# Packed attention and two wide layers on one core: a reciprocal from another pair of ScalarE functions, one wait less, and a new list order

## The chip, the cores and the metric

One core of one Trainium2 chip runs the whole program. The metric is the device time of one execution in microseconds; three executions of the kernel before were timed, and one more was profiled.

## What is computed

Shapes: `q`, `k`, `v` are (8, 8, 576, 64), `p` is (8, 8, 32, 64); both layers have 4608 tokens, width 512 and hidden width 2048, all float32.

```python
p_packed = softmax(p k^T / 8) v              # 32 packed rows per head
x = softmax(q p_packed^T / 8) p_packed       # (4608, 512) after the heads are joined
h = x @ w_in1                                # layer 1
P = a0 + a1*h + a2*h^2 + a3*h^3
Q = 1 + |b0|*|h| + |b1|*h^2
x = (P / (Q + 1e-6)) @ w_out1
h = x @ w_in2                                # layer 2
out = (h * cos(h)) @ w_out2
```

## The kernel before

The program is a list of steps, each with an engine, an assumed duration, a key and the objects it reads and writes. `Plan.order` walks through the list as a model of five engines would: it starts, on each engine, the step with the lowest key among those that could start within 60 ns of the first, and the resulting order is the order in which instructions are recorded. A key is a place in a schedule written by hand (`at`, `FROM + u * UNIT`, ...) plus an entry of the table `WANTED` for its kind of step. So a new table means a new order on every engine; the engines then run their own queues strictly in that order and wait on each other by semaphores.

**Attention** runs in 16 units (`attention`, half the heads of one batch each): loads of `p`, `k`, `q`, `v`; PE transposes (L470); scores (L499); softmax of the packed queries (`exp1`, L517); the product with `v` (L550); the second scores; the second softmax (`exp2`, L590) with VectorE transposes around it; a store of the result.

**Weights** arrive as 64-bit words and are turned into a high and a low float32 part: `w_load` (512 KB), `w_exp` and `w_low` on ScalarE (L359, L362), `w_abs` and `w_join` on VectorE (L368, L378), then for most a rounding on ScalarE (L385) and a subtraction on GpSimd (L390). `raw` has two buffers, so a load waits for the `w_join` two conversions earlier. Layer 1 has 32 such conversions.

**Layer 1** has 128 items (`item1`; 16 token columns by 8 pairs of hidden blocks). The attention matrix is multiplied into the weights first (`m_prod`, L694; `m_hi`, L703; `m_lo`, L707). One item then is: `front` on PE (L739, 12 matmuls of 288 columns); on ScalarE `absolute` (L850), `lin` (L836), `slope` (L853); on GpSimd `denom` (L859); on VectorE `cubic` twice (L845, L847); on ScalarE `rsqrt` (L862) and `square` (L866), which make 1/Q; on VectorE `over` twice (L870) and `ratio` (L874); then `upper` on ScalarE (L902), `lower` on VectorE (L905) and `back` on PE (L776, 24 matmuls). `lower` is the seventh VectorE step of an item and the last thing that its `back` needs. The hidden values sit in one of two PSUM buffers (`b2`), which come free when the second `cubic` has read them; `V` and `U` have three buffers each, `T` four.

`rsqrt` of the first eight items waits for the end of every softmax: in `item1` it has `after=exps if j < 8 else ()`, where `exps` lists all `exp1` and `exp2` steps. `rsqrt` and the exponential are in different table sets of ScalarE.

**Layer 2** has 144 items (`item2`): `front` (L755), `lin` (L838), `rounded`, two `reduced`, `clipped`, `cosine` (L893), `times` (L896), `upper`, `lower`, `back`. Here the PSUM buffer is held until `times` has read it.

Of the kernel before, what the change touches and what calls it, by code (L numbers as in the profile page):

```python
# [14 lines left out]
AF = mybir.ActivationFunctionType  # L15
# [12 lines left out]
class Plan:  # L28
# [13 lines left out]
    WANTED = {  # L42
        "a2_hi": 440, "a2_lo": 373, "a2_load": -22, "absolute": -628, "back 0": 104, "back 1": 169,
        "clipped": 70, "copied k": 251, "copied q": 43, "cosine": 245, "cubic 0": 228,
        "cubic 1": -452, "denom": -187, "done1": -328, "done2": -87, "doubled": 357, "exp1": 189,
        "exp2": 14, "exp_copied 0": -32, "exp_copied 1": 522, "front 0": -261, "front 1": -372,
        "keep_attn": 271, "keep_out": 425, "keep_pack": 48, "less_max2": -596, "lin 0": -168,
        "lin 1": -278, "load k": 275, "load p": -435, "load q": -220, "load v": 93, "lower 0": -109,
        "lower 1": 78, "m_hi": -93, "m_lo": 32, "m_load": -254, "m_prod": -307, "max1": -559,
        "max2": -95, "open_left": -187, "open_right": 541, "over 0": 72, "over 1": 202, "pack": 436,  # L50
        "packed": -313, "ratio": -102, "recip1": 165, "recip2": 77, "reduced 0": 285,
        "reduced 1": -222, "rounded": 209, "rsqrt": 308, "scaled2": 49, "scores 0": -225,
        "scores 1": 191, "slope": -116, "square": -380, "store": 355, "sum2": 21, "taken p": -208,
        "taken pp": 108, "times": -128, "trans k": 275, "trans q": 147, "turn2": 46,
        "turn_back": -404, "turn_exp": 79, "turned p": 64, "turned pp": 562, "upper 0": -141,
# [6 lines left out]
        "x_load": -33, "x_out": -508,  # L62
    }
# [138 lines left out]
def pack_attention_moe_moe_kernel(  # L202
# [14 lines left out]
    nc = tc.nc  # L217
# [23 lines left out]
    ONE_EPS = 1.0 + 1e-6  # L241
    MAGIC = 12582912.0
    C1 = 6.28125
    C2 = 2 * PI - C1
    EARLY = 8
    N1 = NH * NPR
# [62 lines left out]
    add = plan.add  # L309
# [15 lines left out]
    cst = POOL["cp"].tile([P, 4], F32, name="cst")  # L325
# [285 lines left out]
    exps, ld_users, tp_users, ps_users = [], [], [], []  # L611
# [102 lines left out]
    def layer(j):  # L714
        return items[j][0]
# [110 lines left out]
    def shaped(j, nm):  # L826
        t = TILE[nm, j]
        return t.rearrange("p (a b) -> p a b", a=2) if layer(j) == 0 else t[:, 0:CH]
# [31 lines left out]

    def rsqrt(j):
        nc.scalar.activation(shaped(j, "V"), shaped(j, "U"), AF.Abs_reciprocal_sqrt, bias=ONE_EPS)  # L862

    def square(j):
        V = shaped(j, "V")
        nc.scalar.activation(V, V, AF.Square)  # L866

# [8 lines left out]
    def rounded(j):  # L876
        T = shaped(j, "T")
        return nc.vector.tensor_scalar(T, T, MAGIC, MAGIC, op0=ALU.add, op1=ALU.subtract)  # L878

    def reduced(j, e):  # L880
        T, Y = shaped(j, "T"), shaped(j, "U")
        if e == 0:
            return nc.vector.scalar_tensor_tensor(Y, T, -C1, hidden(j), op0=ALU.mult, op1=ALU.add)
        else:
# [27 lines left out]
    def at(j):  # L912
        return BEGIN + (ITEM1 * j if j <= N1 else ITEM1 * N1 + ITEM2 * (j - N1))
# [28 lines left out]
    W2P = ([P, 2 * HS], F32)  # L942
    fronts, rsqrts = {}, []
    HOMES2 = {f: f"s{f}" for f in range(NF // 2)}
# [28 lines left out]
    def item1(j):  # L973
        l, c, i = items[j]
        key = at(j)
# [8 lines left out]
        add("DVE", 730, key, cubic, j, 1, tail=85, r=[("h", j)], w=[("T", j)])  # L984
        rsqrts.append(add("ACT", 590, key, rsqrt, j, tail=105, r=[("U", j)], w=[("V", j)], after=exps if j < 8 else ()))
        add("ACT", 585, key, square, j, tail=100, w=[("V", j)])
        add("DVE", 669, key, over, j, 1, tail=85, r=[("V", j)], w=[("U", j)])
# [27 lines left out]
    def item2(j):  # L1015
        l, c, f = items[j]
        key = at(j)
# [5 lines left out]
        add("DVE", 336, key, clipped, j, tail=85, w=[("U", j)])  # L1023
        add("ACT", 535, key, cosine, j, tail=100, w=[("U", j)], after=rsqrts[-8:] if j < N1 + 8 else ())
        add("DVE", 600, key, times, j, tail=85, r=[("U", j), ("h", j)], new=[("V", ("V", j), *W2P)])
# [14 lines left out]
    for c in range(NH):  # L1040
        operands1(c)
        for i in range(NPR):
            j = c * NPR + i
# [20 lines left out]
    nc.sync.dma_start(par[:, 4:6], rat_b.unsqueeze(0).to_broadcast([P, 2]))  # L1064
    nc.vector.memset(cst[:, 0:1], ONE_EPS)
    nc.vector.memset(cst[:, 1:2], 0.25)
    nc.vector.memset(cst[:, 2:3], PI / 2)
    nc.scalar.activation(par[:, 4:6], par[:, 4:6], AF.Abs)
    for s in plan.order():
# [40 lines left out]
```

## Time and profile before

| | |
|---|---|
| three timed executions | 1664.0, 1664.95, 1667.54 us; median 1664.95 us |
| the profiled execution | 1665.34 us; span from first to last instruction 1663.4 us |
| busy, share of the span | PE 1570.7 us (94%), VectorE 1289.6 us (78%), ScalarE 1021.1 us (61%), GpSimd 308.3 us (19%) |
| mean granted TensorE clock | 0.97 of full speed |

The span is the sum of what an engine does and of what it waits. A stage in which PE is busy all the time is bound by PE; in one where PE waits, the question is which engine's work, or which chain across engines, it waits for. Numbers of rows and columns in names (`128x576`) are partitions by elements. L followed by a number is a line of the kernel before; in the changed kernel the lines after the table of constants are one higher.

### The profile page before, as it was taken

How to read it: one execution, taken by the hardware profiler on the slowest of the kernel's cores; microseconds unless marked ns; L12 is line 12 of the kernel's file. 1: busy time of each engine (PE TensorE's matmuls, PEld its weight loads, DVE VectorE, ACT ScalarE, POOL GpSimd, SP SyncE). 2: the span in 40 equal slices, each digit the busy share in tenths (PEclk: the TensorE clock that was granted, in tenths of full speed). 3: DMA queues.
4: the chain of work that ended last, by engine and by line, in shares of the span. 5: the costliest groups of instructions: out<-in, count | busy, mean ns of one | idle time of the engine just before them, and what ended most of it. 6: DMA issues, size and time to landing. Idle time of an engine off the chain costs nothing.

```text
span 1663.4 us, 26699 instructions
## 1 busy us (share of the span) xinstructions
PE 1570.7 (94%) x10176; PEld 1347.7 (81%) x10176; DVE 1289.6 (78%) x2025; ACT 1021.1 (61%) x1706; POOL 308.3 (19%) x246
## 2 busy tenths in 40 slices
PE   5876579999999999999999999999999999999998
PEld 3444278999999999999998888888888888888887
DVE  2655888999999999999998876667676667576664
ACT  3655788989999889898986543333333334333332
POOL 0233423333333333333322100000000000000000
PEclk7888689999999999999999999999999999999999
DMA  8998441212121121213153210101010100101010
GB/s 254 244 279 241 130 124 36 69 36 75 46 71 64 41 70 54 70 48 132 34 183 104 87 47 13 38 14 38 1 46 12 27 18 20 32 14 38 1 26 26
DMA packets 84383, 120.75 MB, mean 73 GB/s; under 512 B 19232, under 2 KB 61216, under 8 KB 84256
## 3 DMA queue, kind: packets, MB, share of 16 engines
q1 hardware_dynamic: 83872, 118.53, 24.4%
q8 instruction: 80, 1.31, 0.3%
q10 hardware_dynamic: 384, 0.52, 0.1%
q14 instruction: 47, 0.39, 0.1%
HBM read 85.99 MB, written 33.03 MB: 72 GB/s over the span
## 4 chain that ended last, share of the span: by engine, by line
PE 86%; DVE 4%; DMA 4%; ACT 3%; issue 1%; POOL 1%; SPq 1%; POOLq 0%; ACTq 0%
PE acc L776 46%; PE b L755 24%; PE b L739 11%; DMA raw<-in_moe_w_in_dram 2%; PE b L694 2%; PE b L470 1%; DMA v_in<-in_v_dram 1%; DMA raw<-in_moe_w_out_dram 1%; PE b L499 1%; DVE sc L368 1%; DVE T L870 0%; ACT sc L362 0%; DVE U L870 0%; POOL r L602 0%; ACT sc L359 0%
## 5 line engine op out<-in xcount | busy, mean ns | idle before, releaser
L776 PE MATMUL acc<-gh,wo 128*128 128x288 f32 x2048 | 418.0, 298 | 9.0 <-ACT gh L902 9.0
L776 PE MATMUL acc<-wo,gh 128*128 128x512 f32 x1152 | 354.7, 389 | 0.0
L776 PEld LDWEIGHTS acc<-gh,wo 128*128 128x128 f32 x2048 | 331.3, 189 | 26.9 <-issue 15.9
L776 PE MATMUL acc<-gl,wo 128*128 128x288 f32 x1024 | 303.2, 296 | 0.9 <-DVE gl L905 0.7
L776 PEld LDWEIGHTS acc<-wo,gh 128*128 128x128 f32 x1152 | 216.2, 188 | 44.9
L859 POOL TENSOR_TENSOR U<-U,V 128x576 f32<-128x576 f32 x128 | 182.7, 1437 | 361.4 <-DVE T L874 105.5
L776 PE MATMUL acc<-wo,gl 128*128 128x512 f32 x576 | 224.2, 389 | 0.0
L893 ACT ACTIVATE U<-U 128x512 f32<-128x512 f32 x144 | 90.6, 630 | 204.6 <-DVE U L889 204.5
L905 DVE TENSOR_TENSOR gl<-V,gh 128x512 fp32r<-128x512 f32 x144 | 99.2, 689 | 127.6 <-PE acc L776 126.2
L776 PEld LDWEIGHTS acc<-gl,wo 128*128 128x128 f32 x1024 | 194.4, 190 | 2.0 <-DVE gl L905 1.9
L838 ACT ACTIVATE T<-b 128x512 f32<-128x512 f32 x144 | 85.9, 596 | 176.7 <-PE b L755 176.4
L902 ACT CAST gh<-V 128x512 fp32r<-128x512 f32 x144 | 89.4, 621 | 73.4 <-PE acc L776 68.0
L776 PEld LDWEIGHTS acc<-wo,gl 128*128 128x128 f32 x576 | 108.1, 188 | 22.5
L905 DVE TENSOR_TENSOR gl<-T,gh 128x576 fp32r<-128x576 f32 x128 | 111.8, 876 | 7.6 <-PE acc L776 4.7
L878 DVE TENSOR_SCALAR T<-T 128x512 f32<-128x512 f32 x144 | 60.8, 423 | 70.2 <-ACT T L838 69.8
L896 DVE TENSOR_TENSOR V<-U,b 128x512 f32<-128x512 f32 x144 | 98.2, 682 | 18.0 <-ACT U L893 14.4
L853 ACT ACTIVATE U<-V,par 128x576 f32<-128x576 f32 x128 | 111.0, 873 | 0.8 <-DVE T L874 0.7
L870 DVE SCALAR_TENSOR_TENSOR T<-T,par,V 128x576 f32<-128x576 f32 x128 | 105.2, 841 | 5.0 <-ACT V L866 4.9
L836 ACT ACTIVATE T<-b,par 128x576 f32<-128x576 f32 x128 | 106.1, 830 | 3.5 <-PE b L739 3.0
L885 DVE SCALAR_TENSOR_TENSOR U<-T,U 128x512 f32<-128x512 f32 x144 | 103.6, 720 | 4.0
L850 ACT ACTIVATE V<-b 128x576 f32<-128x576 f32 x128 | 82.9, 648 | 35.4 <-PE b L739 26.3
L847 DVE SCALAR_TENSOR_TENSOR T<-T,par,b 128x576 f32<-128x576 f32 x128 | 101.3, 809 | 3.5 <-ACT V L850 1.4
(182 smaller groups left out, 3053.5 us busy)
## 6 DMA issues: line engine op xcount, KB each, us to landing
raw<-in_moe_w_out_dram SPq DMA_DIRECT2D x32, 512.0 KB, 3.7
q_in<-in_q_dram SPq DMA_DIRECT2D x16, 576.0 KB, 5.6
k_in<-in_k_dram SPq DMA_DIRECT2D x16, 576.0 KB, 6.8
x<-ob SPq DMA_DIRECT2D x16, 576.0 KB, 3.5
raw<-in_moe_w_in_dram SPq DMA_DIRECT2D x32, 256.0 KB, 4.3
v_in<-in_v_dram SPq DMA_DIRECT2D x64, 128.0 KB, 6.1
raw<-in_moe_w_in_dram SPq DMA_DIRECT2D x16, 512.0 KB, 4.8
w<-sc SPq DMA_DIRECT2D x32, 256.0 KB, 2.3
```

The lines of the kernel that those rows point to most:

```text
L739: nc.tensor.matmul(TILE["h", j][:, e, 0:HS], lhsT=w[:, o : o + P], rhs=x[:, g, :], start=n == 0, stop=n == 3 * NG - 1,)
L755: nc.tensor.matmul(h, lhsT=w[:, ks], rhs=x, start=n == 0, stop=n == 3 * KC - 1)
L776: nc.tensor.matmul(o, lhsT=w, rhs=x, start=i == 0 and n == 0, stop=i == last and n == len(todo) - 1,)
L836: nc.scalar.activation(T, hidden(j), AF.Identity, scale=par[:, 3:4], bias=par[:, 2:3])
L847: nc.vector.scalar_tensor_tensor(T, T, par[:, 1:2], h, op0=ALU.add, op1=ALU.mult)
L853: nc.scalar.activation(shaped(j, "U"), shaped(j, "V"), AF.Identity, scale=par[:, 5:6], bias=par[:, 4:5])
L859: return nc.gpsimd.tensor_tensor(Q, Q, V, op=ALU.mult)
L870: return nc.vector.scalar_tensor_tensor(t, t, add_, shaped(j, "V"), op0=ALU.add, op1=ALU.mult)
L885: return nc.vector.scalar_tensor_tensor(Y, T, -C2, Y, op0=ALU.mult, op1=ALU.add)
L893: nc.scalar.activation(Y, Y, AF.Sin, bias=PI/2)
L896: nc.vector.tensor_tensor(shaped(j, "V"), shaped(j, "U"), hidden(j), op=ALU.mult)
L905: return nc.vector.tensor_tensor(shaped(j, "gl"), result(j), shaped(j, "gh").bitcast(F32), op=ALU.subtract)
```

## The change

Three things change. The reciprocal: `rsqrt` then `square` become `log` then `inverse`, 1/Q as exp(-ln Q), with Q scaled by 2^-22 ahead of the logarithm and scaled back in the exponential's bias. The wait: `log` no longer has the `after=exps`. The table: every entry of `WANTED` is new, and `exp_copied` has one entry in place of two. A table set that holds logarithm and exponential is named ahead of the program.

```diff
     WANTED = {
-        "a2_hi": 440, "a2_lo": 373, "a2_load": -22, "absolute": -628, "back 0": 104, "back 1": 169,
+        "a2_hi": -487, "a2_lo": 16, "a2_load": -116, "absolute": -171, "back 0": 868,
...
-    def rsqrt(j):
-        nc.scalar.activation(shaped(j, "V"), shaped(j, "U"), AF.Abs_reciprocal_sqrt, bias=ONE_EPS)
-
-    def square(j):
+    def log(j):
+        nc.scalar.activation(shaped(j, "V"), shaped(j, "U"), AF.Ln, scale=2.0**-LOW, bias=cst[:, 0:1])
+
+    def inverse(j):
         V = shaped(j, "V")
-        nc.scalar.activation(V, V, AF.Square)
+        nc.scalar.activation(V, V, AF.Exp, scale=-1.0, bias=cst[:, 3:4])
...
-        rsqrts.append(add("ACT", 590, key, rsqrt, j, tail=105, r=[("U", j)], w=[("V", j)], after=exps if j < 8 else ()))
-        add("ACT", 585, key, square, j, tail=100, w=[("V", j)])
+        logs.append(add("ACT", 590, key, log, j, tail=105, r=[("U", j)], w=[("V", j)], ))
+        add("ACT", 585, key, inverse, j, tail=100, w=[("V", j)])
...
-        add("ACT", 535, key, cosine, j, tail=100, w=[("U", j)], after=rsqrts[-8:] if j < N1 + 8 else ())
+        add("ACT", 535, key, cosine, j, tail=100, w=[("U", j)], after=logs[-8:] if j < N1 + 8 else ())
...
-    nc.vector.memset(cst[:, 0:1], ONE_EPS)
+    nc.scalar.preload_act_table_set("natural_log_exp_and_others")
+    nc.vector.memset(cst[:, 0:1], ONE_EPS * 2.0**-LOW)
...
+    nc.vector.memset(cst[:, 3:4], -LOW * math.log(2.0))
```

What the new table does is seen in the order of the engines. Three places follow; the number behind a name tells one tile from the next of its kind.

**ScalarE, the reciprocal of layer 1's first item.** Before (`V_2347` is the first item's, `V_2359` the second's; `r_2364` is the last unit of attention):

```order
L590 ACTIVATE r_2364<-r_2364 128x576
L862 ACT_TABLE_LOAD
L862 ACTIVATE V_2347<-U_2354 128x576
L359 ACTIVATE sc_2450<-raw_2417 128x512
L362 ACTIVATE sc_2453<-raw_2417 128x512
L866 ACTIVATE V_2347<-V_2347 128x576
L862 ACTIVATE V_2359<-U_2379 128x576
```

In the change (`V_2348` first item, `V_2361` second, `V_2419` third, `r_2372` the last unit):

```order
L863 ACTIVATE V_2348<-U_2356,cst 128x576
L867 ACTIVATE V_2348<-V_2348,cst 128x576
L360 ACTIVATE sc_2412<-raw_2364 128x512
L363 ACTIVATE sc_2415<-raw_2364 128x512
L851 ACTIVATE V_2419<-b_1_2397 128x576
L837 ACTIVATE T_2425<-b_1_2397,par 128x576
L854 ACTIVATE U_2428<-V_2419,par 128x576
L863 ACTIVATE V_2361<-U_2383,cst 128x576
L867 ACTIVATE V_2361<-V_2361,cst 128x576
L591 ACTIVATE r_2372<-r_2372 128x576
```

The reciprocals of the first two items now stand ahead of the last exponential of attention, and no table load stands between them. Over the whole program ScalarE has three table loads before (at the start, here, and at the first cosine) and two now (at the start and at the first cosine).

**VectorE, the first item's `ratio` and `lower`.** Before (`T_2351` is the first item's, `sc` and `s` are weight conversions):

```order
L874 SCALAR_TENSOR_TENSOR T_2351<-U_2354,T_2351 128x576
L368 SCALAR_TENSOR_TENSOR sc_2519<-sc_2516,sc_2519 128x512
L870 SCALAR_TENSOR_TENSOR U_2379<-U_2379,V_2359 128x576
L378 SCALAR_TENSOR_TENSOR s_2533<-raw_2483,sc_2519 128x512
L905 TENSOR_TENSOR gl_2535<-T_2351,gh_2528 128x576
```

In the change (`T_2352` is the first item's, `T_2367` the second's, `T_2425` the third's):

```order
L871 SCALAR_TENSOR_TENSOR U_2356<-U_2356,V_2348 128x576
L379 SCALAR_TENSOR_TENSOR s_2417<-raw_2332,sc_2392 128x512
L369 SCALAR_TENSOR_TENSOR sc_2415<-sc_2412,sc_2415 128x512
L871 SCALAR_TENSOR_TENSOR T_2352<-T_2352,par,V_2348 128x576
L379 SCALAR_TENSOR_TENSOR s_2417<-raw_2364,sc_2415 128x512
L875 SCALAR_TENSOR_TENSOR T_2352<-U_2356,T_2352 128x576
L846 TENSOR_TENSOR T_2367<-T_2367,b_0_2335 128x576
```

The first item's `ratio` moves from the 44th to the 27th VectorE instruction, counted from the first `m_lo`; its `lower` moves from the 48th to the 46th, because one conversion (two instructions) less stands ahead of it. From the first `m_lo` to the tenth `lower` there are 121 VectorE instructions in either order, of the same kinds but for one `ratio` less and one `over` more; 16 conversions stand among them in both.

**SyncE, the last load of `q`.** Before:

```order
L448 DMA v_in_1958<-in_v_dram 32x4x256 x4
L450 DMA v_in_1958<-in_v_dram 32x4x64 x2
L454 DMA q_in_1975<-in_q_dram 128x1152
L351 DMA raw_1987<-in_moe_w_out_dram 128x512
L568 DMA ppt_99<-lhpp_2012 128x128
```

In the change:

```order
L449 DMA v_in_1950<-in_v_dram 32x4x256 x4
L451 DMA v_in_1950<-in_v_dram 32x4x64 x2
L352 DMA raw_1958<-in_moe_w_out_dram 128x512
L455 DMA q_in_1999<-in_q_dram 128x1152
L569 DMA ppt_99<-lhpp_1995 128x128
L352 DMA raw_2051<-in_moe_w_out_dram 128x512
```

A weight load now stands ahead of the last load of attention: 15 weight loads of 512 KB come before it where there were 14. In layer 2 the new order also records two `front` steps with no `back` between them 39 times, where the order before does so 29 times.

## Rows read from the trace of the kernel before

**Rows 1.** The page, busy time of each engine over the span, with instructions.

```profile
PE 1570.7 (94%) x10176; PEld 1347.7 (81%) x10176; DVE 1289.6 (78%) x2025; ACT 1021.1 (61%) x1706; POOL 308.3 (19%) x246
```

**Rows 2.** Stretches: length, busy time (instructions) by engine, clock, DMA share, GB/s.

```profile
core 0: us, PE busy (x) PEld busy (x) DVE busy (x) ACT busy (x) POOL busy (x), PEclk, DMA share, GB/s
0.00:160.00 160.00, 108.28 (x1438) 69.04 (x1438) 79.52 (x177) 90.10 (x182) 37.60 (x51) 0.83 0.94 262
160.00:176.00 16.00, 10.36 (x164) 5.04 (x170) 10.59 (x19) 10.19 (x21) 8.19 (x7) 0.70 0.37 109
176.00:211.00 35.00, 15.85 (x106) 9.87 (x90) 31.76 (x49) 26.37 (x40) 12.96 (x11) 0.70 0.49 130
211.00:273.00 62.00, 51.01 (x360) 46.50 (x360) 53.02 (x72) 51.43 (x84) 22.86 (x17) 0.91 0.31 94
273.00:860.00 587.00, 586.73 (x4567) 561.35 (x4566) 563.07 (x760) 533.42 (x849) 205.99 (x146) 1.00 0.21 69
860.00:1600.00 740.00, 740.00 (x3298) 608.36 (x3298) 519.29 (x898) 291.79 (x505) 20.70 (x16) 1.00 0.13 34
1600.00:1664.00 64.00, 58.44 (x258) 47.50 (x256) 32.32 (x56) 17.76 (x30) 0.00 (x0) 0.98 0.06 17
```

**Rows 3.** Timeline of PE around the first back: start, us, work [idle before <-releaser].

```profile
198.55 1.95 PE L694 MATMUL b<-s,pt 64*32 64x512 f32 x10 [3.46 <-DVE s L378]
209.49 0.85 PE L776 MATMUL acc<-gh,wo 128*128 128x288 f32 x2 [9.00 <-ACT gh L902]
211.06 0.61 PE L776 MATMUL acc<-gl,wo 128*128 128x288 f32 x1 [0.72 <-DVE gl L905]
...
242.72 0.84 PE L739 MATMUL b<-a,m00h 128*128 128x288 f32 x2 [5.64 <-ACT V L850]
```

**Rows 4.** Timeline of GpSimd: the first item's denominator.

```profile
185.61 1.41 POOL L859 TENSOR_TENSOR U<-U,V 128x576 f32<-128x576 f32 x1
```

**Rows 5.** Timeline of ScalarE: the end of attention's softmax and the first reciprocal.

```profile
196.41 0.67 ACT L590 ACTIVATE r<-r 128x576 f32<-128x576 f32 x1
197.10 1.28 ACT L862 ACT_TABLE_LOAD   x1
198.39 0.68 ACT L862 ACTIVATE V<-U 128x576 f32<-128x576 f32 x1
```

**Rows 6.** Timeline of VectorE: first low part, two waits, the first and tenth lower.

```profile
175.98 1.23 DVE L707 TENSOR_TENSOR m00l<-b,m00h 128x1024 fp32r<-128x1024 f32 x1 [0.83 <-ACT m00h L703]
...
200.22 0.69 DVE L368 SCALAR_TENSOR_TENSOR sc<-sc,sc 128x512 uint32<-128x512 uint32 x1 [1.34 <-ACT sc L362]
...
210.25 0.75 DVE L905 TENSOR_TENSOR gl<-T,gh 128x576 fp32r<-128x576 f32 x1
...
247.25 0.76 DVE L905 TENSOR_TENSOR gl<-T,gh 128x576 fp32r<-128x576 f32 x1 [1.25 <-ACT gh L902]
...
274.07 0.76 DVE L905 TENSOR_TENSOR gl<-T,gh 128x576 fp32r<-128x576 f32 x1
```

**Rows 7.** Groups by line on ScalarE: count | busy us, mean ns | idle before.

```profile
L853 ACT ACTIVATE U<-V,par 128x576 f32<-128x576 f32 x128 | 111.0, 873 | 0.8 <-DVE T L874 0.7
L866 ACT ACTIVATE V<-V 128x576 f32<-128x576 f32 x128 | 86.8, 685 | 1.9
L862 ACT ACTIVATE V<-U 128x576 f32<-128x576 f32 x128 | 86.5, 685 | 10.5 <-POOL U L859 9.8
L590 ACT ACTIVATE r<-r 128x576 f32<-128x576 f32 x16 | 10.9, 684 | 4.7 <-POOL r L586 4.5
```

**Rows 8.** Groups by line on VectorE in 176 to 211 us: the conversions.

```profile
L368 DVE SCALAR_TENSOR_TENSOR sc<-sc,sc 128x512 uint32<-128x512 uint32 x7 | 4.9, 701 | 2.1 <-ACT sc L362 2.1
L378 DVE SCALAR_TENSOR_TENSOR s<-raw,sc 128x512 uint32<-128x512 uint32 x7 | 4.7, 682 | 0.0
```

**Rows 9.** Waits: who waited for whom, us in total, times, longest us.

```profile
PEld b L755 <- DVE V L896: 10.5, 56, 0.4
```

**Rows 10.** The page, DMA issues: KB each, us from issue to landing.

```profile
raw<-in_moe_w_out_dram SPq DMA_DIRECT2D x32, 512.0 KB, 3.7
```

More of the change, by code (lines that the diff above doesn't have):

```diff
@@ L42 @@
     WANTED = {
-        "a2_hi": 440, "a2_lo": 373, "a2_load": -22, "absolute": -628, "back 0": 104, "back 1": 169,
[L44 to L54, printed above, removed]
@@ L55 @@
-        "turn_back": -404, "turn_exp": 79, "turned p": 64, "turned pp": 562, "upper 0": -141,
[6 rows of a table removed]
-        "x_load": -33, "x_out": -508,
+        "a2_hi": -487, "a2_lo": 16, "a2_load": -116, "absolute": -171, "back 0": 868,
+        "back 1": 414, "clipped": -39, "copied k": 50, "copied q": 379, "cosine": 427,
+        "cubic 0": 2184, "cubic 1": 373, "denom": -324, "done1": -240, "done2": 222, "doubled": 65,
+        "exp1": 12, "exp2": 366, "exp_copied": 1828, "front 0": -75, "front 1": 28, "inverse": -39,
@@ new lines @@
+        "keep_attn": -193, "keep_out": -663, "keep_pack": 344, "less_max2": -839, "lin 0": -40,
+        "lin 1": -157, "load k": -100, "load p": 127, "load q": -16, "load v": -216, "log": 1940,
+        "lower 0": -199, "lower 1": -193, "m_hi": 303, "m_lo": -7, "m_load": -209, "m_prod": -122,
+        "max1": 209, "max2": -574, "open_left": 194, "open_right": -121, "over 0": 590,
+        "over 1": 442, "pack": -397, "packed": 485, "ratio": 235, "recip1": 303, "recip2": -376,
+        "reduced 0": 499, "reduced 1": 387, "rounded": -296, "scaled2": -170, "scores 0": -545,
@@ L63 @@
+        "scores 1": 7, "slope": 61, "store": 293, "sum2": -213, "taken p": 487, "taken pp": -300,
+        "times": 372, "trans k": 320, "trans q": -206, "turn2": 432, "turn_back": 314,
+        "turn_exp": 342, "turned p": 160, "turned pp": 85, "upper 0": -564, "upper 1": 392,
[5 rows of a table added]
+        "w_low 1 i": 264, "w_low 1 o": 185, "x_hi": 547, "x_lo": -435, "x_load": 274,
+        "x_out": -308,
     }
@@ L242, in pack_attention_moe_moe_kernel @@
     MAGIC = 12582912.0
+    LOW = 22
     C1 = 6.28125
@@ L942, in pack_attention_moe_moe_kernel @@
     W2P = ([P, 2 * HS], F32)
-    fronts, rsqrts = {}, []
+    fronts, logs = {}, []
     HOMES2 = {f: f"s{f}" for f in range(NF // 2)}
```

11 rows, old and new, of the table WANTED are left out of this document.

## The prediction

> **What bounds the kernel now.** Read the page's busy line first: PE works 1570.7 of 1663.4 us [rows 1], so all that any reordering can win lies in the 92.7 us in which PE stands still, and in what its clock loses. Then read the table of stretches, which says where those 92.7 us are [rows 2]. From 273 to 1600 us PE is busy for 1326.73 of 1327 us at the full clock: no other engine can shorten that part, and it can only start earlier. The tail from 1600 us to the span's end holds 5.0 us of idle PE (the last output copies and stores) and has the same work in either kernel. The first 160 us hold 51.7 us, but there the DMA engines are 94% busy at 262 GB/s with attention's loads: that stage is bound by transfers of which the change removes none. What is left is 160 to 273 us: 5.6 us up to 176, then 19.2 us up to 211, then 11.0 us up to 273.
>
> Who is late there? PE waits 9.00 us for the first item's rounded result before its first `back` and 5.64 us later for an `absolute` [rows 3]. Behind both stands VectorE: from the first low part at 176 us to 273 us it is busy 84.8 of 97 us, in order 31.76 of 35 and 53.02 of 62 [rows 2]. So it idles 12.2 us, 3.2 in the first piece and 9.0 in the second, and these are the only microseconds that a different order of the same work can take out of this stage. This is the number the forecast hangs on, rather than the more striking 9.00 us of PE.
>
> **The removed wait.** The first item's denominator is done on GpSimd at 185.61 + 1.41 = 187.0 us [rows 4], and its `rsqrt` starts at 198.39 us, after the last exponential and a table load [rows 5]. So one chain is held 11.4 us. That is not what the program gains. VectorE had other work: in the 35 us up to the first `lower` it idled only 3.2 us, and that `lower` stands behind 47 instructions before and 45 now. The ratio comes earlier, but what it overtakes (conversions, the third and fourth item's `cubic`) must still be done ahead of the tenth `lower`, and up to there both orders hold 121 VectorE instructions of practically the same kinds. The wait's removal is worth at most the idle time that it causes.
>
> **The table load.** It goes: 1.28 us on ScalarE, directly between two activations, 1.31 us from the end of the exponential (197.08) to the start of `rsqrt` [rows 5]. A conversion stands behind it, and VectorE waits 1.34 us for a conversion right there, at 200.22 [rows 6]; so this is part of the 3.2 us and is not counted again. The Trainium skill (ScalarE: Activation LUTs, What ACT_TABLE_LOAD costs) gives about 2.66 us for a change of set, with a drain of 1.38 us; no drain is to be seen here, the gap is 1.31 us in all. By the page the sum below would be 1.4 us lower, 1658.6 us.
>
> **The two functions.** `log` and `inverse` replace `rsqrt` and `square` one for one, 128 each, in shape 128x576. The exponential has a row: 684 ns, against 685 ns for `rsqrt` and 685 ns for `square` [rows 7]. The logarithm has none. Bounds: 684 ns, the nearest row, a table function of the same shape from SBUF; and 873 ns, `slope`, which takes both operands per partition where these take only the bias. Below 684 no row of this shape from SBUF lies, so no gain is assumed. I take 685, hence 0, because the functions read from a table agree to 1 ns and what differs in `slope` is the scale. At 873 it would be 2 x 188 ns an item: over the ten items up to 273 us 3.8 us of ScalarE, which idled 19.2 us in that stretch, and over the other 118 some 44 us, against 53.6 us that ScalarE idles from 273 to 860 us [rows 2]. So even that end is mostly hidden; I keep +3.8 us for it.
>
> **The order of attention's loads.** A 512 KB weight load moves ahead of the last load of `q`, and queues it, a `ppt` store and the stores behind it on SyncE's queue. 512 KB at 262 GB/s [rows 2] are 2.0 us of a saturated queue; alone such a load lands in 3.7 us [rows 10]. If the end of attention hangs on that load, everything after it is 2.0 us late. If not, it costs 0: between 160 and 176 us the DMA engines are 37% busy, and the last units still have VectorE, ScalarE and PE steps to go through, so a part is covered. I take +1.0 us, half, as no row tells where between the ends it lies. The same stretch could also get shorter, since VectorE idles 5.4 of its 16 us; half of that, 2.7 us, is kept for the low end and nothing for the sum, because what waits there is one unit's own chain of steps, which the change leaves as it is.
>
> **The work up to the first `lower`.** One conversion less, 701 + 682 ns on VectorE [rows 8], moves behind it: 1.4 us for the first `back`, but by the tenth `lower` it has been made up (121 against 121). It moves when PE starts, not when PE is saturated. 0 in the sum.
>
> **VectorE's idle time, first piece (3.2 us).** Of it 2.1 us were waits for a conversion's ScalarE step [rows 8], and those steps stood behind the table load and the four reciprocals that were released together at 198 us. With reciprocals spread from about 187 us on, I take 2.5 of the 3.2 us as gone.
>
> **Second piece (9.0 us).** These are short waits, many of them for a ScalarE step that in turn waited for VectorE's `over` or `ratio`: the 1.25 us for an `upper` at 247.25 is one [rows 6]. They come from items that pass in groups, and the new order still groups the fifth to seventh item, so most of the pattern stays. From both sides: 0 and 9.0. I take 3.5, nearer the low end.
>
> **Sum.** +1.0 - 2.5 - 3.5 + 0 = -5.0 us. The profiled execution took 1665.34 us, 0.4 above the median of the three runs (1664.95): 1660.3 against its own time, 1660.0 on the scale of the median. Nothing gives it back later: after saturation PE has no gaps to grow into as long as VectorE (563 of 587 us busy up to 860) keeps up, and it has the same work there.
>
> **Rivals.** *Hidden anyway.* VectorE's idle time only changes its place: other waits in the group of the fifth to seventh item, which now begin after a first `back` that comes earlier, take the 6 us. For it: 121 instructions against 121, and ScalarE at 51.43 of 62 us. Against it: the table load and the burst of four are gone for certain. Time: between no gain with 1.0 us of later loads, 1666, and 3 us of gain, 1662; middle 1664.
>
> *Slower: layer 2's PSUM buffers.* In layer 2 a buffer is held from `front` to `times`. Already PE's weight loads wait for `times` 56 times, 0.4 us at the longest [rows 9], hidden under running matmuls: the stage has 740.0 of 740 us busy [rows 2] but little to spare. The new order puts two fronts in a row 39 times instead of 29, which fills both buffers. If each such pair shows the longest of these waits, PE loses 39 x 0.4 = 15.6 us, net 1660.0 + 15.6 = 1675.6. It decides from 0.21 us a pair (8.3 us: the 5.0 gained and 3.3 more). Against it: 29 pairs cost nothing in this trace, and VectorE is busy only 519 of 740 us.
>
> *The change doesn't do what it says.* If logarithm and exponential were served by different sets, each pair would reload: 256 x 1.28 us on ScalarE, hundreds of us. The order shows two loads in all, so I give this nothing.
>
> *Larger gain.* All 12.2 us of idle go, the loads cost nothing, and attention's last stretch gives 2.7 us: 1665.0 - 12.2 - 2.7 = 1650.1; without the last term 1652.8.
>
> **Chances.** A measurement of this kernel can tell 0.2%, 3.3 us, from no change: faster means under 1661.6, slower over 1668.3. The forecast with the larger gain: 0.55 (0.47 and 0.08). Hidden: 0.30, all within the 3.3 us. Slower: 0.15, of which the buffers 0.08, and 0.07 for dearer functions (+3.8) or the full 2.0 us of the loads together with no idle time won. The range leaves out little of the larger gain and most of the slower cases: from 1650.0, where every idle microsecond goes, to 1669.0, the median with 3.8 us of dearer functions and nothing won.
>
> **What would show it.** The first `log` at about 187 to 190 us, and no table load near it. The first `back` at 205 to 209 us instead of 209.49. VectorE's idle time between the first `m_lo` and the tenth `lower` down from 12.2 to about 6 us; that is the step I am least sure of. PE busy without a gap from about 268 us. `log` and `inverse` at 685 ns. Layer 2 at 740 of 740 us. The prediction is wrong if VectorE still idles 12 us there, if attention ends over 2 us later, or if PE shows gaps after 300 us.

## The result: slower by 0.55%, and the profile after

The changed kernel takes 1674.7 us (median of 4 runs, 1672.86 to 1676.01) where the kernel before took 1664.9 beside it: ratio 1.0055, 95% interval 1.0038 to 1.0073. The forecast was 1660.0 with a range up to 1669; it was wrong in sign. The profiled execution took 1673.76 us, with a span of 1672.0 us against 1663.4 before.

The page of the kernel after, busy time of each engine over the span; it answers to [rows 1]:

```profile
PE 1573.5 (94%) x10176; PEld 1351.4 (81%) x10176; DVE 1282.3 (77%) x2026; ACT 1038.6 (62%) x1705; POOL 308.3 (18%) x246
```

PE has the same 10176 matmuls and 2.8 us more busy time, VectorE 7.3 us less. ScalarE has 17.5 us more, although a table load and its 1.28 us are gone. The groups by line on ScalarE of the kernel after (count | busy us, mean ns | idle before us) say from where:

```profile
L854 ACT ACTIVATE U<-V,par 128x576 f32<-128x576 f32 x128 | 111.5, 876 | 0.4 <-DVE T L875 0.2
L867 ACT ACTIVATE V<-V,cst 128x576 f32<-128x576 f32 x128 | 98.8, 779 | 1.9
L863 ACT ACTIVATE V<-U,cst 128x576 f32<-128x576 f32 x128 | 98.1, 779 | 16.7 <-POOL U L860 16.1
```

`log` (L863) and `inverse` (L867) take 779 ns each, where `rsqrt` and `square` took 685 [rows 7]. The stretches of the kernel after, in the columns of [rows 2], with the long piece cut at 302 and at 900 us:

```profile
160.00:176.00 16.00, 10.25 (x121) 4.96 (x121) 11.09 (x19) 8.89 (x17) 7.98 (x7) 0.57 0.43 133
176.00:211.00 35.00, 18.30 (x117) 13.77 (x118) 33.23 (x53) 28.53 (x44) 13.56 (x11) 0.72 0.54 146
211.00:273.00 62.00, 51.31 (x355) 46.23 (x354) 51.34 (x69) 52.32 (x83) 21.42 (x16) 0.85 0.20 67
273.00:302.00 29.00, 29.00 (x236) 27.38 (x235) 28.06 (x39) 26.95 (x40) 11.24 (x8) 1.00 0.25 74
302.00:860.00 558.00, 555.00 (x4308) 529.12 (x4307) 526.15 (x717) 518.35 (x803) 193.44 (x137) 1.00 0.21 68
900.00:1600.00 700.00, 700.00 (x3062) 571.37 (x3062) 477.53 (x833) 264.83 (x455) 11.62 (x9) 1.00 0.11 29
1600.00:1672.00 72.00, 65.35 (x287) 53.16 (x285) 37.86 (x65) 19.64 (x34) 0.00 (x0) 0.98 0.07 18
```

and the same cuts of the kernel before:

```profile
273.00:302.00 29.00, 28.92 (x223) 26.65 (x222) 28.02 (x39) 26.51 (x41) 11.16 (x8) 0.96 0.17 52
302.00:860.00 558.00, 557.80 (x4346) 534.70 (x4345) 535.04 (x722) 506.91 (x809) 194.83 (x139) 1.00 0.21 70
900.00:1600.00 700.00, 700.00 (x3076) 572.78 (x3075) 481.97 (x840) 264.80 (x457) 11.64 (x9) 1.00 0.11 30
1600.00:1663.40 63.40, 58.44 (x258) 47.50 (x256) 32.32 (x56) 17.76 (x30) 0.00 (x0) 0.98 0.06 17
```

Do not read the busy time here, read the number behind the x. Between 900 and 1600 us PE is busy for 700.00 of 700 us in both, and yet it issues 14 matmuls fewer after: at 700 / 3076 = 0.228 us each, 3.2 us are lost with no idle time on record, because a matmul that starts late behind one still running counts as busy. Between 302 and 860 us it issues 38 fewer, at 558 / 4346 = 0.128 us, 4.9 us, of which only 2.8 us show as idle; it is nearer 6 us, because 17 of the kernel before's 4346 are layer 2's first matmuls, of 512 columns instead of 288, and the kernel after has issued none of those by 860 us. At 1600 us the kernel after has 65.35 - 58.44 = 6.9 us of PE's work more to do, and its tail holds 6.65 idle us against 4.96: together the 8.6 us by which its span is longer.

The 1.7 idle us that the tail has more come from one wait. The last output copy on ScalarE, before and after, from the timelines:

```profile
1658.03 0.58 ACT L795 COPY sc<-acc 128x512 f32<-128x512 f32 x1 [1.01 <-PE acc L776]
```

```profile
1666.48 0.59 ACT L796 COPY sc<-acc 128x512 f32<-128x512 f32 x1 [2.55 <-DMA out_dram<-sc]
```

Before, it waits for the matmuls that it copies; after, for an earlier store out of `sc`, and the last stores start that much later.

The start went as forecast, up to a point. Timeline of PE of the kernel after, around the first `back`, beside [rows 3]:

```profile
204.92 0.85 PE L777 MATMUL acc<-gh,wo 128*128 128x288 f32 x2 [5.23 <-ACT gh L903]
206.38 0.61 PE L777 MATMUL acc<-gl,wo 128*128 128x288 f32 x1 [0.60 <-DVE gl L906]
```

and of VectorE: the first `m_lo`, the first and the tenth `lower`, beside [rows 6]:

```profile
174.93 1.23 DVE L708 TENSOR_TENSOR m00l<-b,m00h 128x1024 fp32r<-128x1024 f32 x1 [0.50 <-ACT m00h L704]
...
205.57 0.75 DVE L906 TENSOR_TENSOR gl<-T,gh 128x576 fp32r<-128x576 f32 x1
...
272.96 0.76 DVE L906 TENSOR_TENSOR gl<-T,gh 128x576 fp32r<-128x576 f32 x1
```

The first `back` comes 4.6 us earlier. But from the first `m_lo` to the tenth `lower` it is 98.03 us, and was 98.09. The busy times of those two pieces, in the columns of the stretches, of the kernel before and then of the kernel after:

```profile
175.98:210.25 34.27, 15.79 (x106) 9.87 (x90) 31.03 (x47) 26.39 (x40) 12.98 (x11) 0.70 0.48 126
210.25:274.07 63.82, 52.09 (x364) 47.23 (x364) 54.73 (x75) 52.50 (x86) 22.86 (x17) 0.90 0.31 95
```

```profile
174.93:205.57 30.64, 13.55 (x99) 9.14 (x98) 29.38 (x45) 26.58 (x42) 14.63 (x12) 0.77 0.56 145
205.57:272.96 67.39, 56.09 (x372) 50.82 (x372) 56.22 (x77) 55.30 (x88) 21.42 (x16) 0.82 0.22 72
```

VectorE idled 3.2 + 9.1 = 12.3 us before and idles 1.3 + 11.2 = 12.4 us after. The idle time moved from the first piece into the second.

PE nevertheless came out of the start ahead. Count its matmuls in the order in which they start: the 2300th starts at 304.70 us before and at 301.54 after, 3.2 us earlier. Of this, 1.05 us is the earlier first `m_lo`; the other 2.1 us are won on the way from there, without any less idle time of VectorE. The 6600th, at the end of layer 1, starts 3.1 us later than before. So layer 1 turned a lead of 3.2 us into a delay of 3.1.

### The profile page after: what moved, and what is told of

Its sections match the earlier page's. It is cut to its first block, busy times and chain, and to the rows that moved or that the text cites. A ratio compares the mean times of both kernels' runs of the same rounds, so it can differ in the third digit from the quotient of the medians.

```text
span 1672.0 us, 26696 instructions
## 1 busy us (share of the span) xinstructions
PE 1573.5 (94%) x10176; PEld 1351.4 (81%) x10176; DVE 1282.3 (77%) x2026; ACT 1038.6 (62%) x1705; POOL 308.3 (18%) x246
## 4 chain that ended last, share of the span: by engine, by line
PE 75%; ACT 9%; DVE 7%; DMA 4%; issue 2%; POOL 1%; SPq 0%; ACTq 0%; DVEq 0%; POOLq 0%
PE acc L777 39%; PE b L756 24%; PE b L740 8%; PE b L695 2%; ACT T L837 1%; ACT V L867 1%; ACT V L863 1%; DMA raw<-in_moe_w_out_dram 1%; DMA k_in<-in_k_dram 1%; PE b L471 1%; ACT V L851 1%; ACT U L854 1%; DVE U L871 1%; ACT gh L903 1%; DMA v_in<-in_v_dram 1%
## 5 line engine op out<-in xcount | busy, mean ns | idle before, releaser
L903 ACT CAST gh<-V 128x512 fp32r<-128x512 f32 x144 | 89.5, 622 | 125.9 <-PE acc L777 116.3
L897 DVE TENSOR_TENSOR V<-U,b 128x512 f32<-128x512 f32 x144 | 98.5, 684 | 35.1 <-ACT U L894 30.9
L871 DVE SCALAR_TENSOR_TENSOR U<-U,V 128x576 f32<-128x576 f32 x128 | 100.8, 797 | 15.6 <-ACT V L867 14.0
L863 ACT ACTIVATE V<-U,cst 128x576 f32<-128x576 f32 x128 | 98.1, 779 | 16.7 <-POOL U L860 16.1
L906 DVE TENSOR_TENSOR gl<-T,gh 128x576 fp32r<-128x576 f32 x128 | 104.2, 817 | 4.9 <-PE acc L777 3.8
L846 DVE TENSOR_TENSOR T<-T,b 128x576 f32<-128x576 f32 x128 | 93.1, 746 | 13.1 <-ACT T L837 12.1
## 6 DMA issues: line engine op xcount, KB each, us to landing
v_in<-in_v_dram SPq DMA_DIRECT2D x64, 128.0 KB, 5.5
```

Source lines behind the costliest of these rows:

```text
L863: nc.scalar.activation(shaped(j, "V"), shaped(j, "U"), AF.Ln, scale=2.0**-LOW, bias=cst[:, 0:1])
L871: return nc.vector.scalar_tensor_tensor(t, t, add_, shaped(j, "V"), op0=ALU.add, op1=ALU.mult)
L897: nc.vector.tensor_tensor(shaped(j, "V"), shaped(j, "U"), hidden(j), op=ALU.mult)
L903: nc.scalar.copy(shaped(j, "gh"), result(j))
L906: return nc.vector.tensor_tensor(shaped(j, "gl"), result(j), shaped(j, "gh").bitcast(F32), op=ALU.subtract)
```

## The experiments

Three parts of the change can be taken apart: the two functions with their operands, the removed wait, and the table. Times below are medians with the ratio to the kernel before on the same chip.

Before the experiments, a word on how far one profile can be trusted. Two executions of one and the same kernel (the version in the second experiment with plain numbers) began their first `m_lo` at 177.78 and at 173.95 us, with spans of 1663.4 and 1659.7 us: the part up to there alone moves a span by 3.8 us. Why it does is not shown. The DMA engines were 90% and 89% busy up to 178 us, and the granted clock was 0.79 in the first and 0.83 in the second; the timed runs of this version go the same way, from 1660.98 us at a mean clock of 0.973 to 1666.42 at 0.968, and which of the two, transfers or clock, leads was not tested. From the first `m_lo` to the end the two took 1485.6 and 1485.8 us. So profiles are compared by that length, which I call the **run after attention**: 1663.4 - 175.98 = 1487.4 us before, 1672.0 - 174.93 = 1497.1 after.

### The biases as plain numbers, all else as changed

```diff
-        nc.scalar.activation(shaped(j, "V"), shaped(j, "U"), AF.Ln, scale=2.0**-LOW, bias=cst[:, 0:1])
+        nc.scalar.activation(shaped(j, "V"), shaped(j, "U"), AF.Ln, scale=2.0**-LOW, bias=ONE_EPS * 2.0**-LOW)
...
-        nc.scalar.activation(V, V, AF.Exp, scale=-1.0, bias=cst[:, 3:4])
+        nc.scalar.activation(V, V, AF.Exp, scale=-1.0, bias=-LOW * math.log(2.0))
```

> The changed kernel, its order untouched; only the two biases of log and inverse are given as plain numbers instead of a column of the constants tile. Theory A (a per-partition operand costs some 94 ns an activation, and in layer 1 ScalarE cannot hide 128 x 2 x 94 ns = 24 us): both activations take 685 ns instead of 779, PE keeps the 3.0 us of lead that it has at 302 us until layer 1 ends, where the changed kernel lay 2.6 us behind, and the time is about 1674.7 - 5.6 = 1669 us. Theory B (the new order alone makes the loss, ScalarE hides the dearer activations): 685 ns, but the time stays at 1673 to 1676 us. Layer 2 is as in the changed kernel under either.

1667.1 us, ratio 1.0012 (1.0001 to 1.0023). Its groups on ScalarE:

```profile
L867 ACT ACTIVATE V<-V 128x576 f32<-128x576 f32 x128 | 86.7, 684 | 1.8
L863 ACT ACTIVATE V<-U 128x576 f32<-128x576 f32 x128 | 86.3, 685 | 18.6 <-POOL U L860 18.2
```

and its stretches:

```profile
302.00:860.00 558.00, 557.32 (x4332) 532.78 (x4332) 531.88 (x724) 504.96 (x806) 193.41 (x137) 1.00 0.22 72
900.00:1600.00 700.00, 700.00 (x3063) 571.38 (x3062) 476.52 (x832) 262.54 (x451) 10.55 (x8) 1.00 0.11 28
```

So it is not logarithm and exponential that are dear, it is the column they read: 94 ns for a bias given as one value per partition. With the order unchanged the columns add 256 x 94 ns = 24 us of instructions to ScalarE (18.3 us of busy time, 1020.3 to 1038.6, since neighbours overlap), and they cost 1.0055 - 1.0012 = 0.0043, about 7 us of time (the intervals leave 4 to 11). Layer 1 gets 24 of its 38 missing matmuls back. Layer 2, which has neither function, gets one: its loss belongs to the order.

### The order of before with the new functions, once with columns and once with plain numbers

```diff
-        logs.append(add("ACT", 590, key, log, j, tail=105, r=[("U", j)], w=[("V", j)], ))
+        rsqrts.append(add("ACT", 590, key, rsqrt, j, tail=105, r=[("U", j)], w=[("V", j)], after=exps if j < 8 else ()))
```

and `WANTED` as it was before; the steps keep their old names in it and hold logarithm and exponential. With columns:

> The kernel before in its own order, with its wait for attention's end, but with logarithm and exponential as the change writes them (biases from the constants tile, the table set named ahead of the program). Theory A: 779 ns each, layer 1 loses some 5.6 us as in the changed kernel, less 1.3 us for the table load that goes: about 1669 us. Theory B: the kernel before hides them, 1663 to 1665 us.

With plain numbers:

> The kernel before in its own order, wait kept, with logarithm and exponential whose biases are plain numbers: only the functions and the table load differ from before. Both theories: 685 ns each; 0 to 1.3 us faster than before, 1663.6 to 1665 us. If it is as slow as the changed kernel, the logarithm is dear for another reason.

With columns 1666.2 us, ratio 1.0007 (0.9996 to 1.0018), functions at 778 and 777 ns. With plain numbers 1663.0, ratio 0.9989 (0.9977 to 1.0001), functions at 685 ns; once more, below, 1663.2 and 0.9992 (0.9983 to 1.0001). So the functions with their saved table load are worth about 1.5 us, just at the edge of what shows. The columns cost 0.0018, 3 us, in this order (the intervals leave 0.3 to 5.7); the run after attention says the same, 1488.6 against 1485.6. That may be less than the 7 us in the new order, but the intervals overlap.

### The wait removed, the table of before

```diff
-        rsqrts.append(add("ACT", 590, key, rsqrt, j, tail=105, r=[("U", j)], w=[("V", j)], after=exps if j < 8 else ()))
+        rsqrts.append(add("ACT", 590, key, rsqrt, j, tail=105, r=[("U", j)], w=[("V", j)], ))
```

against the version just told, with logarithm, exponential, plain numbers and the table of before.

> Logarithm and exponential with plain numbers as biases, no wait for attention's end, and the old table of list offsets (the entries of rsqrt and square, for kinds that no longer exist under these names here, apply as before): the wait's removal without the new table. Theory B (the new table is at fault in layers 1 and 2): 1660 to 1663 us, some 3 us gained ahead of 300 us and none given back. Theory A says the same of layer 1 and nothing of layer 2: 1660 to 1665 us. If removing the wait is itself what spoils the order, 1668 us or more.

1679.9 us, ratio 1.0088 (1.0069 to 1.0108): 17 us worse than the same kernel with its wait. The tenth `lower` comes 106.2 us after the first `m_lo`, 8.1 us later than before, and VectorE idles 19 us up to there. VectorE's timeline shows at the first `lower` a wait of 3.72 us, put down to a transfer, where neither the kernel before nor the one after waits at all:

```profile
211.44 1.43 DVE L906 TENSOR_TENSOR gl<-T,gh 128x576 fp32r<-128x576 f32 x2 [3.72 <-DMA a<-a2T]
```

A table belongs to one list: without its wait the planner makes another order of it. This run therefore does not price the wait alone, only the wait together with a table made for it.

### The wait kept, the new table

```diff
-        logs.append(add("ACT", 590, key, log, j, tail=105, r=[("U", j)], w=[("V", j)], ))
+        logs.append(add("ACT", 590, key, log, j, tail=105, r=[("U", j)], w=[("V", j)], after=exps if j < 8 else ()))
```

with plain numbers as biases; a few dozen instructions of each of PE, VectorE and ScalarE move.

> The changed kernel with plain numbers as biases, and the first eight logarithms held back again until attention's last exponential; the new table as it is. Theory that the removed wait only moves VectorE's idle time: VectorE stands idle about 12 us between the first low part of the tables and the tenth item's rounding, as in every version so far, the first `back` comes about 4 us later, and the time is 1667 us within 1.5. Rival, that the removed wait is worth what I forecast: 1670 to 1672 us.

1666.2 us, ratio 1.0005 (0.9992 to 1.0017), against 1.0012 (1.0001 to 1.0023) without the wait: no difference that can be told. By the two intervals the wait's removal lies between a gain of 1.7 us and a loss of 4; and the run with the wait has the short tail of the kernel before (its last output copy waits 1.01 us, for PE), where the run without it has the long one (2.54 us, for a store), so that 1.6 us between the two belong to neither. My own detail missed: the first `back` did not come 4 us later; the first `lower` stands 30.5 us after the first `m_lo`, as without the wait (30.9). The new table ends the softmax sooner, with the last exponential at 192.86 us. VectorE's idle time up to the tenth `lower` is 11.6 us, as expected. What the change was named for, that no item waits for attention's end, is worth nothing that can be told here.

### Layer 2 by the entries of before

```diff
     WANTED = {
...
-        "back 1": 414, "clipped": -39, "cosine": 427, "front 1": 28, "lin 1": -157, "lower 1": -193,
-        "reduced 0": 499, "reduced 1": 387, "rounded": -296, "times": 372, "upper 1": 392, "done2": 222,
+        "back 1": 169, "clipped": 70, "cosine": 245, "front 1": -372, "lin 1": -278, "lower 1": 78,
+        "reduced 0": 285, "reduced 1": -222, "rounded": 209, "times": -128, "upper 1": -40, "done2": -87,
...
```

against the version with plain biases; the entries of `x_load`, `x_hi`, `x_lo`, `store`, `w_back` and of the conversions of the second output weights go back in the same way (the lines show only entries that change). Attention and layer 1 stand in the order of the change.

> The changed kernel with plain numbers as biases, and with the table of before for the kinds of layer 2; attention and layer 1 stand in the same order as in the version with plain biases (1667.1 us). Theory that layer 2's new order creeps without any idle time showing: between 900 and 1600 us it issues about 3076 matmuls, as before, in place of 3063, and the 2 to 4 us come back: 1662 to 1664 us, ratio to before 0.998 to 0.999. Rival, that the creep comes from when the items arrive or from layer 1's order: 3063 matmuls again, 1667 us.

1665.0 us, ratio 0.9994 (0.9984 to 1.0005), about 3 us less than with the new order of layer 2 (the intervals leave 0.5 to 5.5). Between 900 and 1600 us it issues 3070 matmuls where that one issues 3063 and the kernel before 3076, and its tail is as short as before. The time is 1 to 3 us above what the theory asked. The version with the wait kept, which has the new order of layer 2 and ran beside this one, lies only 1.8 us above it, and the intervals leave -0.8 to 4.5.

One profile of each, cut at the same matmuls, says where the microseconds lie. The columns are the lengths in us from the first instruction to the first `m_lo`, from there to the start of the 2300th matmul, on to the 6600th (layer 1), to the 6900th (the change to layer 2), to the last, and from that to the end:

| version | first `m_lo` | to 2300th | to 6600th | to 6900th | to last | tail |
|---|---|---|---|---|---|---|
| kernel before | 176.0 | 128.7 | 551.0 | 56.4 | 745.9 | 5.4 |
| order of before, plain numbers | 177.8 | 127.4 | 550.8 | 56.4 | 745.7 | 5.4 |
| order of before, columns | 174.2 | 127.9 | 553.3 | 56.4 | 745.7 | 5.3 |
| the change | 174.9 | 126.6 | 557.2 | 56.9 | 749.3 | 7.0 |
| plain numbers | 173.5 | 125.9 | 552.7 | 57.0 | 749.1 | 6.8 |
| plain numbers, wait kept | 174.6 | 127.0 | 551.8 | 57.0 | 749.5 | 5.3 |
| plain numbers, layer 2 by the entries of before | 176.2 | 125.2 | 552.2 | 58.4 | 747.2 | 5.4 |
| two columns (told below) | 172.1 | 128.0 | 569.5 | 57.0 | 749.6 | 6.9 |

Every version with layer 2's new order takes 749.1 to 749.6 us from the 6900th matmul to the last, every one with the whole order of before 745.7 to 746.1 (a repeat told below included): that order costs some 3.4 us there. Layer 2's old entries behind the new order of layer 1 give back 1.9 of them, but lose 1.4 in the change from layer 1 to layer 2; the two other versions with a mixed order, told above and below, have 58.8 and 58.7 us there too. Of the 3 us that the old entries are worth against the version with plain numbers, about half is the tail, which the version with the wait has short even with layer 2's new order.

How the new order of layer 2 loses time shows in the timeline of the weight loads of the kernel after, between 1300 and 1330 us:

```profile
1307.91 1.24 PEld L756 LDWEIGHTS b<-x,s 128*128 128x128 f32 x6 [0.28 <-DVE V L897]
1315.58 1.23 PEld L756 LDWEIGHTS b<-x,s 128*128 128x128 f32 x6 [0.28 <-DVE V L897]
1325.36 1.23 PEld L756 LDWEIGHTS b<-x,s 128*128 128x128 f32 x6 [0.39 <-DVE V L897]
```

and of its matmuls, two `front` steps in a row:

```profile
1305.18 1.52 PE L756 MATMUL b<-x,s 128*128 128x512 f32 x6
1306.54 0.84 PE L756 MATMUL b<-ob,s 128*128 128x512 f32 x3
1307.22 0.84 PE L756 MATMUL b<-raw,s 128*128 128x512 f32 x3
1307.92 1.67 PE L756 MATMUL b<-x,s 128*128 128x512 f32 x6
1309.42 0.86 PE L756 MATMUL b<-ob,s 128*128 128x512 f32 x3
```

The first `front` goes from its first to its second weight in 1306.54 - 1305.18 = 1.36 us, the second in 1309.42 - 1307.92 = 1.50: its weight load had to wait until `times` (L897) freed the PSUM buffer, and 0.14 us of that came through. In the kernel before, the same waits are more but shorter. Waits of PE's weight loads between 900 and 1600 us, before and after (us in total, times, longest):

```profile
PEld b L755 <- DVE V L896: 9.6, 51, 0.4
```

```profile
PEld b L756 <- DVE V L897: 7.7, 25, 0.4
PEld acc L777 <- DVE xr L794: 1.6, 6, 0.3
```

Short waits cost little, but not nothing. One of the kernel before:

```profile
983.84 0.53 PEld L755 LDWEIGHTS b<-ob,s 128*128 128x128 f32 x3 [0.17 <-DVE V L896]
```

```profile
983.93 0.88 PE L755 MATMUL b<-ob,s 128*128 128x512 f32 x3
984.64 0.86 PE L755 MATMUL b<-raw,s 128*128 128x512 f32 x3
```

Its three matmuls take 984.64 - 983.93 = 0.71 us where others take 0.68 (1306.54 to 1307.22 above). The price of each wait can be taken as the time from the start of the matmul before it to the start of the matmul behind, less twice the usual distance of 0.227 us. Over all waits between 900 and 1600 us: before, 46 waits of up to 0.20 us cost 0.02 us each and five of 0.30 to 0.38 us 0.18 each, 1.9 us in all. After, 24 waits for `times` of 0.27 to 0.39 us cost 0.16 us each and the six for an output copy, which are new, 0.12 each, 4.7 us in all. The difference, 2.8 us, is nearly all of the 3.2 us.

### Two columns

```diff
-        nc.scalar.activation(shaped(j, "V"), shaped(j, "U"), AF.Ln, scale=2.0**-LOW, bias=cst[:, 0:1])
+        nc.scalar.activation(shaped(j, "V"), shaped(j, "U"), AF.Ln, scale=cst[:, 4:5], bias=cst[:, 0:1])
...
-        nc.scalar.activation(V, V, AF.Exp, scale=-1.0, bias=cst[:, 3:4])
+        nc.scalar.activation(V, V, AF.Exp, scale=cst[:, 5:6], bias=cst[:, 3:4])
```

> The changed kernel with the factors of logarithm and exponential as columns too, so that each of the 256 functions reads two columns where the change has one and the version with plain biases none; the order is the same. Theory that ScalarE pays about 94 ns for each column: 873 to 876 ns each, 24 us more of ScalarE, and between 302 and 860 us fewer matmuls again; the first column cost 7.6 us of time, so 1682 us or more, as the slack left is smaller. Rival, that it is the functions with a bias from memory that are slow and not the column: 779 ns and 1674 us.

1684.9 us, ratio 1.0111 (1.0091 to 1.0131). Its groups on ScalarE:

```profile
L854 ACT ACTIVATE U<-V,par 128x576 f32<-128x576 f32 x128 | 111.1, 873 | 0.4 <-DVE T L875 0.2
L867 ACT ACTIVATE V<-V,cst 128x576 f32<-128x576 f32 x128 | 110.5, 870 | 1.9
L863 ACT ACTIVATE V<-U,cst 128x576 f32<-128x576 f32 x128 | 109.7, 870 | 15.7 <-POOL U L860 15.5
```

and its longest stretch of layer 1:

```profile
302.00:860.00 558.00, 547.76 (x4222) 518.31 (x4221) 516.56 (x698) 524.14 (x785) 190.59 (x136) 1.00 0.20 66
```

685, 779, 870 ns for no column, one and two: a column costs 91 to 94 ns whether it is factor or bias, and `slope` at 873 ns is the same function with two. The matmuls issued there go 4332, 4308, 4222. The first column cost 0.0043 of the time and the second 0.0056. ScalarE is busy 505, 518 and 524 of 558 us; it never fills the stretch, and yet some 9 of the last 23 us reach the end.

### Attention by the new entries, the layers by those of before

```diff
     WANTED = {
...
-        "exp1": 189, "exp2": 14, "less_max2": -596, "load k": 275, "load p": -435, "load q": -220, "load v": 93,
+        "exp1": 12, "exp2": 366, "exp_copied": 1828, "less_max2": -839, "load k": -100, "load p": 127, "load q": -16, "load v": -216,
...
```

against the order of before with logarithm, exponential, plain numbers and the wait, and so on for all of attention's kinds of steps (the lines show only entries that change); beside it that version itself, run again.

> The kernel of before with logarithm and exponential (plain numbers as biases) and its wait, and of the new table only the entries of attention's kinds of steps; layers 1 and 2 keep the entries of before. Theory that attention's new order ends it earlier, as five profiles of the new table show (first low part of the tables at 172.1 to 176.2 us, against 174.2 to 177.8 in four of the old): first low part near 174.5 us, and 1 to 1.5 us less than with the old order, about 1661.5 us, ratio 0.998. Rival, my term of +1.0 for the loads' order, or no difference beyond the scatter of the loads: 1663 to 1664.5 us, ratio 0.999 to 1.0.

> The kernel of before with logarithm and exponential and plain numbers as biases, its order and its wait as they were; run again beside the version with attention's new order. Expected as measured the first time: 1663 us, ratio 0.999, that is the 1.2 us of the one table load that goes; with attention's new order theory it is 1 to 1.5 us above the other.

1670.0 us, ratio 1.0029 (1.0016 to 1.0041), against 1663.2 and 0.9992. Both theories missed. The first `m_lo` did come at 174.48 us, but layer 1 lost it and more (4309 matmuls between 302 and 860 us, for 4343 in the run beside it): half a table is no table, as in the third experiment. Whether the new order of attention ends it sooner stays open: first `m_lo` at 172.1 to 176.2 us in six profiles with it, 174.0 to 177.8 in five without.

## Why the prediction was wrong

**The two functions** is the step that failed by most: of the 9 us by which the kernel is slower, 7 are theirs. With plain numbers it would have been no change, though still not the gain that I forecast. I took 0 and argued that what differs in `slope` is the scale, and that even the dear end "is mostly hidden", for ScalarE idles 53.6 us between 273 and 860 us; I kept 3.8 us, from the ten items of the start alone. Both halves failed. `slope` reads two columns and costs 188 ns more than `square` [rows 7]; half of that for each was the plain reading, and 779 ns is what was measured. And 24 us more on an engine with over 50 idle us cost 7 us, because idle time that lies elsewhere does not cover a step in an item's chain. The row that goes with it is VectorE's wait for the end of `inverse` (us in total, times, longest), between 302 and 860 us with plain numbers and then with the column:

```profile
DVE U L871 <- ACT V L867: 5.5, 11, 1.8
```

```profile
DVE U L871 <- ACT V L867: 10.5, 22, 2.0
```

With two columns it is 19.0 us, 37 times. The Trainium skill had the price: ScalarE: Activation LUTs, What ACT_TABLE_LOAD costs, gives about 93 ns for each such operand, and this case's 685, 779 and 870 ns agree. My prediction drew on that section for the table load and left this sentence out.

**VectorE's idle time, second piece.** I took 3.5 of 9.0 us as gone; it grew by 2.1, and by 0.6 with plain numbers. The rival *hidden anyway* described it: idle time changes its place. That VectorE's idle time measures what PE can win was itself wrong: it stayed at 12.4 us, and PE still won 2.1 us between the first `m_lo` and the 2300th matmul, where I forecast 6.0. Some 1.4 us the order of before wins there too, once it has logarithm, exponential and plain numbers (127.4 and 127.2 us in its two profiles, for 128.7). The first piece went nearly as said, 2.0 us for 2.5, and so did the outward sign, a first `back` at 204.92 us (forecast 205 to 209, so even a little earlier). But a first `back` that comes sooner is not worth its lead: counted from the first `m_lo` it is 3.5 us early (29.99 us for 33.51), and the tenth `lower` 0.1.

**The removed wait.** That it would not be worth its 11.4 us was right; so was the first `log`, at 187.56 us with no table load near it. It was worth nothing that can be told.

**Nothing gives it back later** was wrong. The row "1326.73 of 1327 us busy" [rows 2] was read as if PE could not be slower there. It hid 3.2 us in layer 2, where my sign "740 of 740 us" came true and meant nothing. And layer 1 lost 6 us: the sign that I named for being wrong, gaps of PE after 300 us, came with 3.0 idle us between 302 and 860 us. The tail, which I took as the same in either kernel, grew by 1.7 us.

**Slower by layer 2's PSUM buffers** was the right mechanism at a fifth of its price. 39 pairs at 0.4 us made 15.6; 3.2 us were lost, 0.08 us a pair, below the 0.21 from which it would have decided alone. With plain numbers it would have left the kernel 2 us over the time before, no change; together with the columns the kernel is slower. That its 1675.6 us lie so near the measured 1674.7 is luck: the columns and the tail, which this rival does not have, fill the gap.

**The order of attention's loads.** The +1.0 us cannot be found: the first `m_lo` came 1.05 us earlier, inside the 3.8 us by which one kernel scatters. Such terms were below what one profile can tell.

What the change is made of, by ratios: functions and table load -1.5 us (at the edge), removed wait nothing that can be told, new order some 3.5 us over that of before, columns +7 us. By the two profiles of the new order with plain numbers, it wins 0.3 to 1.4 us in the start and loses 1 to 2 in layer 1, 0.6 in the change to layer 2 and 3 to 4 in layer 2; the tail costs another 1.5 us in the one without the wait. Open is why layer 2's old entries lose 1.4 us at the change of layers behind the new order of layer 1, what in the order brings the long tail, and which steps make layer 1 itself lose 14 matmuls with plain numbers.

No version beats the kernel before by more than can be told. The best is the old order with its wait, logarithm and exponential, and plain numbers: 1663.0 and 1663.2 us, ratios 0.9989 and 0.9992, with intervals that end at 1.0001.

## What to carry to other kernels

Count the operands of an added instruction that are read from memory, not only its function and shape, and price each by two rows that differ in just that; and multiply by every item of the loop, not by the few at the place one is looking at. When an engine is busy all the time, compare how many instructions it issued in the same stretch of both kernels, or when each starts the same numbered one, before believing that nothing was lost. A table of an order tuned for one list should be changed only as a whole, and the parts of a change should be run one by one even where they were written as one.

## What the runs showed of the hardware

A ScalarE instruction of 128x576 takes 685 ns with plain numbers, 779 with one column and 870 to 876 with two. A weight load's wait for a PSUM buffer is mostly covered while it is short: 46 waits of up to 0.20 us cost the 128x512 matmuls 0.02 us each, 24 of 0.27 to 0.39 us cost them 0.16 each. The end of attention differs by 3.8 us between two executions of one kernel, at granted clocks of 0.79 and 0.83 up to there, while the rest of the program, in that pair, repeats within 0.2 us.
